# Sums of squares taken along with the first projections, and seven more score units for VectorE

## The chip, the cores and the metric

The kernel runs on one core of a Trainium2 chip. A core has a matrix engine (TensorE, "PE" in the profile, with its weight loads as "PEld"), an elementwise engine (VectorE, "DVE"), an activation engine (ScalarE, "ACT"), a general engine (GpSimd, "POOL") and an engine that only issues transfers (SyncE, "SP"). Each works through its own instructions in order; semaphores join them. Sixteen DMA engines move data between DRAM and the on-chip memory SBUF; products of TensorE land in eight banks of PSUM. The metric is the device time of one execution in microseconds.

## What is computed

Two layers, each an attention block and then a gated block, with a layer norm ahead of each, on x of 2048 tokens by 448 features. Both layers use the same weights.

```python
def _A_ref(x, wqkv, wo):                       # 16 heads of 28
    q, k, v = (x @ wqkv) split into heads
    p = softmax(q k^T * 28 ** -0.5)
    return concat(p v) @ wo
def _B_ref(x, w_gate, w_up, w_down):           # 448 -> 1792 -> 448
    return (sigmoid(x @ w_gate) * (x @ w_up)) @ w_down

x = x + _A_ref(_layernorm(x), wqkv, wo)
x = x + _B_ref(_layernorm(x), w_gate, w_up, w_down)
x = x + _A_ref(_layernorm(x), wqkv, wo)
x = x + _B_ref(_layernorm(x), w_gate, w_up, w_down)
```

## The kernel before, in words

**Numbers in two halves.** The result has to be that of fp32 products. TensorE is given each operand as a high and a low fp16 part, and the products high·high, high·low and low·high are added. So that a weight fits fp16, it is scaled by a power of two that follows from the sum of squares of the whole matrix. These sums are `sums[:, 0:3]` for q, k and v, and `sums[:, 3:7]` for wo, w_gate, w_up and w_down. The first three are taken at the very start. The last four, and the fp16 parts of those four matrices, are needed only behind the first attention.

**Projections** (`project`, L678). Tokens come in four blocks of 512. For a block, `qk` (L691) forms seven tiles of 128 rows of q and k, each a chain of 11 matmuls of 512 columns in one of four PSUM banks in turn (L707). ScalarE and VectorE evacuate a tile: high part (L722), low part (L723), squares (L725) and their pairwise maximum (L727). SP writes the parts to DRAM (L730). Three tiles later TensorE takes the tile's norm products, which read those maxima (L701, L704); `finish` (L736) takes the last three and VectorE reduces the peaks (L740). `vals` (L749) forms the values of a block, four tiles of tokens, evacuated by ScalarE (L758).

The lists given to `qk` (`fill`, L731) and `vals` (`after`) set what is put between the tiles, on whichever engine: one entry behind each tile. Here stands the preparation of later blocks. Blocks 2 and 3 are normalised and transposed in 32 x 32 pieces by VectorE (`squares`), stored to DRAM by SP in pieces of 128 fp32 (`store`, L317, tensor `xt_scr`), read back feature by feature (`gather`, L325, tile `xraw`), and split into high and low by ScalarE and VectorE (`ready`, L210 to L216). In layer 0, block 2 is gathered behind tile 0 of block 1, its split stands behind tile 5 and 6, and block 3 is stored behind tile 6. Block 3 is gathered with the first values of block 1 and split behind tiles 1 and 2 of block 2.

Behind the projections a guard is worked out from the peaks (`guard_of_norms`, L836; `worst_of_heads`, L852). All engines read its flag for a branch, and then the first head's operands are completed (L658) and the attention begins.

**Attention** (`attend`, L1101). Work is in units: one key tile of 128 by 512 queries, so 64 units a head and 1024 in all. TensorE forms a unit's scores (L1129). Most units go in groups of three to ScalarE, which takes their exponential in one instruction (`score`, L1133 to L1144). A few are set aside for VectorE, which takes the exponential with some ten instructions on a polynomial (`score_aside`, L1146 to L1163). `FEW` (L66) says how many of each head of layer 0; a head of layer 1 gives three. `ASIDE` says at which key tile a unit is begun, and which one it is. Then TensorE multiplies the probabilities by the values (`mix`, L1180). Behind each key tile `along` is called with its number c, counted from 0 to 255 over the heads.

**Preparing the later weights** (`Prepare`, L912). From c = 4 of layer 0 on, `Prepare` works through a list of steps, each due at a number c. First come 12 raw tiles of wo, w_down, w_gate and w_up, read from DRAM through GpSimd's queue and summed by VectorE: 19 sums of squares (`add`, L1015 to L1020). Then `sizes` (L1031) reduces them over the partitions on GpSimd and works out the scales. Then the matrices are read a second time and split (`split`, L1040), and the parts go to DRAM. The steps of the sums are due every 4 or 5 key tiles, those of the splits every 7 or 8, and the last at c = 220.

**Buffers.** SBUF is cut into 19 large slots and 12 quarter slots. `big.get` takes the slot that has been free longest, `big.put` gives it back at the end of the list (`Slots`, L75). A tile in a slot waits for whoever used the slot last, whatever that was.

Of the kernel before, what the change touches and what calls it, by code (L numbers as in the profile page):

```python
# [11 lines left out]
F32 = mybir.dt.float32  # L12
# [53 lines left out]
FEW = "2221212111111233"  # L66
# [44 lines left out]
def interleaved_layers(ctx: ExitStack, tc: tile.TileContext, x_in, wqkv, wo, w_gate, w_up,  # L111
# [566 lines left out]
    def project(layer, wq, begun):  # L678
# [12 lines left out]
        def qk(b, blk, fill, before):  # L691
# [16 lines left out]
            for i in range(7):  # L708
# [24 lines left out]
                if i < len(fill) and fill[i]:  # L733
                    fill[i]()
# [150 lines left out]
        return values, heads, last_values  # L885

# [25 lines left out]
    class Prepare:  # L912


        def __init__(self):
            nc.vector.memset(sums[:, 3:7], 0.0)
            self.part = cpool.tile([P, 2], F32, name="part", tag="part", bufs=1)
            self.raws, self.packs = big.ring(2), big.ring(2)
            self.halves, self.half = None, 0
            tiles = [("o", 0)] + [("d", j) for j in range(4)] + [("gu", j) for j in range(7)]  # L920
# [3 lines left out]
            self.read(*tiles[0])  # L924
            self.steps = deque()
            at = 6
            for i, (do, what) in enumerate(order):
                then = order[i + 1][1] if i + 1 < len(order) else None
                self.steps.append((at, lambda do=do, what=what, then=then:
                                   self.step(do, what, then)))  # L930
                at += ((5 if what[0] == "gu" else 4) if do == self.measure else
                       {"o": 5, "w": 8}.get(what[0], 7))
                if i == len(tiles) - 1:
                    self.steps.append((at, self.sizes))
# [12 lines left out]
        def read(self, kind, j):  # L947
# [9 lines left out]
            elif kind == "gu":  # L957
# [836 lines left out]
```

## Time and profile before

| | us |
|---|---|
| median of three runs (lowest, highest) | 1913.93 (1912.98, 1913.96) |
| the profiled execution | 1918.24 |
| its span, first to last instruction | 1916.4 |
| TensorE busy | 1897.9 (99%) |
| VectorE busy | 1412.8 (74%) |
| ScalarE busy | 1366.0 (71%) |
| GpSimd busy | 240.6 (13%) |

The granted clock of TensorE is 0.997 on average over the span. The columns of the profile's rows are explained where they are shown. Matmuls overlap in the pipeline, so the length of one is more than the distance from one to the next, and "busy" is no proof that TensorE does all it could.

### The profile page before, as it was taken

Reading aid. Unit: us, or ns where it says so; the run is one execution under the profiler, and the core shown is the slowest. Engines: PE = TensorE matmul, PEld = TensorE weight load, DVE = VectorE, ACT = ScalarE, POOL = GpSimd, SP = SyncE. Lnnn points to the kernel's source line nnn. Section 1 sums busy time; section 2 is a strip of 40 time slices with the busy share of each in tenths; the row PEclk is TensorE's granted clock in tenths of the full one; section 3 lists DMA queues with packets and bytes.
Section 4 is the critical chain, followed back from the end, with each engine's and each line's share of the span. In section 5 each row is a group of like instructions: output and inputs, shape, how many; then the busy total and the mean of one; then the engine's idle time right before and its main releaser. Section 6 shows DMA issues by size and latency. Waiting matters only on the chain. (4 is left out here: it accounts for less than half of the span.)

```text
span 1916.4 us, 56353 instructions
## 1 busy us (share of the span) xinstructions
PE 1897.9 (99%) x24317; PEld 1405.8 (73%) x24317; DVE 1412.8 (74%) x2816; ACT 1366.0 (71%) x1742; POOL 240.6 (13%) x467
## 2 busy tenths in 40 slices
PE   9999999999999999999999999999999999999999
PEld 4455655555566798999954568778888777899998
DVE  7648798687877598788663487778778667887764
ACT  5569999999983455454344799999999645555541
POOL 2013312232001111212100000000000011211110
PEclk9999999999999999999999999999999999999999
DMA  5575555345313657656634312122111235665752
GB/s 173 165 207 162 155 157 149 117 144 149 92 62 92 235 189 263 219 221 236 232 94 132 89 51 51 28 51 51 41 37 66 75 98 215 216 270 198 270 204 90
DMA packets 107298, 275.20 MB, mean 144 GB/s; under 512 B 12766, under 2 KB 63086, under 8 KB 106912
## 3 DMA queue, kind: packets, MB, share of 16 engines
q0 software_dynamic: 33088, 165.74, 24.5%
q1 hardware_dynamic: 73616, 105.54, 19.3%
q8 instruction: 192, 3.15, 0.7%
q14 instruction: 66, 0.54, 0.1%
q10 hardware_dynamic: 336, 0.23, 0.0%
HBM read 213.39 MB, written 50.73 MB: 138 GB/s over the span
## 5 line engine op out<-in xcount | busy, mean ns | idle before, releaser
L1144 ACT ACTIVATE prob_s<-sc 128x1536 f32<-128x1536 f32 x659 | 892.7, 1484 | 6.7 <-PE sc L1129 3.3
L1180 PE MATMUL acc<-prob_s,val_s 128*32 128x256 f32 (+3 forms) x7754 | 590.1, 383 | 0.0
L1129 PE MATMUL sc<-qp_s 114*32 114x512 f16 x7896 | 575.8, 379 | 0.0
L545 PEld LDWEIGHTS <-gu_s 128*128 128x128 f16 x4368 | 428.0, 98 | 60.3 <-issue 8.1
L1129 PEld LDWEIGHTS <-qp_s 114*32 114x32 f16 x8192 | 309.9, 96 | 176.3 <-issue 78.2
L1180 PEld LDWEIGHTS acc<-prob_s,val_s 128*32 128x32 f32 x7754 | 317.9, 110 | 100.8 <-issue 7.6
L545 PE MATMUL chain<-xwide_s,gu_s 128*128 128x256 f16 x2016 | 249.0, 273 | 4.1 <-DMA gu_s<-gu_parts 4.0
L1454 PE MATMUL dnp<-dn_s,hparts_s 128*128 128x224 f16 x2100 | 235.5, 259 | 0.0
L1454 PEld LDWEIGHTS <-hparts_s 128*128 128x128 f16 x2100 | 202.1, 98 | 4.8
L1527 ACT COPY one_q<-chain 128x256 f32<-128x256 f32 x224 | 82.0, 372 | 132.0 <-PE chain L545 131.3
L1160 DVE SCALAR_TENSOR_TENSOR power_q<-power_q,expo_q 128x512 f32<-128x512 f32 x222 | 153.7, 692 | 7.6
L545 PE MATMUL side<-xshort_s,gu_s 128*128 128x256 f16 x1120 | 142.1, 274 | 3.0 <-DVE one_q L1543 2.7
L530 PE MATMUL qkp<-xhl_s,wqk_s 128*128 128x512 f16 x616 | 138.0, 379 | 0.7 <-DVE xhl_s L509 0.3
L1543 DVE TENSOR_TENSOR one_q<-side,one_q 128x512 f32<-128x512 f32 x112 | 72.0, 684 | 83.4 <-PE side L545 83.4
L530 PEld LDWEIGHTS <-wqk_s 128*128 128x128 f16 x616 | 60.0, 98 | 70.1 <-ACT wqk_s L223 1.0
L1209 DVE STREAM_TRANSPOSE oturned_q<-acc 128x512 f32<-128x512 f32 x32 | 22.9, 717 | 118.4 <-PE acc L1180 118.4
L1345 POOL DMA_DIRECT2D gu_s<-gu_parts x104 | 56.0, 540 | 365.7 <-PE side L545 183.3
L545 PE MATMUL side<-xwide_s,gu_s 128*128 128x256 f16 x672 | 92.3, 274 | 0.0
L1407 ACT CAST hparts_s<-hsums_q 128x256 f16<-128x256 f32 (+1 forms) x144 | 68.4, 489 | 33.1 <-DVE hsums_q L1419 20.6
L722 ACT ACTIVATE qkhl_q<-qkp 128x512 f16<-128x512 f32 x56 | 33.2, 593 | 75.0 <-PE qkp L530 71.6
L1180 PE MATMUL acc<-power_q,val_s 128*32 128x256 f32 (+3 forms) x278 | 86.4, 393 | 0.0
L1554 ACT ACTIVATE one_q<-one_q 128x512 f32<-128x512 f32 x56 | 35.3, 630 | 71.3 <-DVE one_q L1543 71.2
(209 smaller groups left out, 2291.0 us busy)
## 6 DMA issues: line engine op xcount, KB each, us to landing
gu_s<-gu_parts POOLq DMA_DIRECT2D x104, 800.0 KB, 6.0
dn_s<-dn_parts POOLq DMA_DIRECT2D x50, 784.0 KB, 7.2
qp_s<-qk_scr SPq DMA_DIRECT2D x96, 224.0 KB
qk_scr<-qkhl_q SPq DMA_DIRECT2D x56, 256.0 KB
gu_parts<-pack_s POOLq DMA_DIRECT2D x14, 800.0 KB, 4.2
xt_scr<-xs_s SPq DMA_DIRECT2D x48, 224.0 KB
xraw_s<-xt_scr SPq DMA_DIRECT2D x12, 768.0 KB
qp_s<-qk_scr SPq DMA_DIRECT2D x64, 112.0 KB
```

Source lines behind the costliest of these rows:

```text
L530: nc.tensor.matmul(pm, w, x, start=(i == 0), stop=(i == len(terms) - 1))
L545: nc.tensor.matmul(pm, a, x, start=(first and i == 0), stop=(i == len(terms) - 1), skip_group_check=True)
L1129: nc.tensor.matmul(ps[32 * j:32 * j + 32, :], hd.k[:, keys], hd.q[:, qb * W:(qb + 1) * W], start=True, stop=True, tile_position=(0, 32 * j))
L1144: nc.scalar.activation(prob[:, 0:n, :], ps[:, 0:n, :], AF.Exp, scale=exp_scale)
L1160: nc.vector.scalar_tensor_tensor(p, p, c[k], y, op0=ALU.add, op1=ALU.mult)
L1180: nc.tensor.matmul(acc[qb * VC:(qb + 1) * VC, s], v[:, kc % TB, h, :], probs[c * NB + qb][:, s], start=(kc == 0 and a == 0), stop=(kc == N ...
L1345: queue.dma_start(self.gu[-1][m], gu_parts[p, m])
L1407: nc.scalar.copy(to[:, :, 0], a)
L1454: nc.tensor.matmul(pm, a[:, x, t], w[:, p, y], start=(begin and n == 0 and (j == 0 or alone)), stop=(n == 2), skip_group_check=True)
L1527: nc.scalar.copy(to, pm)
L1543: nc.vector.tensor_tensor(one[m], side[m], one[m], op=ALU.add)
L1554: nc.scalar.activation(out, v, AF.Sigmoid, scale=gate_scale)
```

## The change

Three things change, all in layer 0.

- The 19 sums of squares leave `Prepare` for a new class `Measure`, used in `project`. Its raw tiles are read through GpSimd's queue, the first four behind tiles 2 to 5 of block 1, the others as a summed tile is given back. One sum stands behind each of two values tiles of block 1, seven behind the tiles of block 2 (one, one, two, none, none, one, two), seven behind those of block 3, and three behind values tiles of blocks 2 and 3. The split of block 3 moves from behind tiles 1 and 2 of block 2 to behind tiles 3 and 4.
- `Prepare` has only `sizes`, due at c = 6, and the splits from c = 7 on, now 11 key tiles apart for w_down and 10 for w_gate and w_up; the last is due at c = 229.
- `FEW` gives VectorE two units in each of the first 15 heads and three in the last, 33 units where there were 26.

```diff
-FEW = "2221212111111233"
+FEW = "2222222222222223"
...
         if layer == 0:
-            fill = [b2.gather, b3.norm, sq(3, 0, 1), sq(3, 2, 3), idle,
-                    lambda: b2.ready(0, 1), lambda: (b2.ready(2, 3), b3.store())]
+            tell = Measure()
+            read, add = tell.read, tell.add
+            two = lambda: add(2)
+            fill = [b2.gather, b3.norm, (read, sq(3, 0, 1)), (read, sq(3, 2, 3)), read,
+                    (read, lambda: b2.ready(0, 1)), (lambda: b2.ready(2, 3), b3.store)]
...
-        vals(1, b1, {0: b3.gather, 2 if layer == 0 else 1: fin})
-        fin = qk(2, b2, [idle, lambda: b3.ready(0, 1), lambda: b3.ready(2, 3)], None)
-        fin = qk(3, blks[3], [], fin)
+        if layer == 0:
+            vals(1, b1, {0: b3.gather, 1: add, 2: fin, 3: add})
+            fin = qk(2, b2, [add, add, two, lambda: b3.ready(0, 1), lambda: b3.ready(2, 3), add,
+                             two], None)
+            fin = qk(3, blks[3], [add, add, add, add, add, add, add], fin)
...
-        vals(2, blks[2], {0: guard_of_norms, 3: worst_of_heads})
+        after = {2: add} if layer == 0 else {}
+        vals(2, blks[2], {0: guard_of_norms, 3: worst_of_heads, **after})
...
-        vals(3, blks[3], {}, range(2))
+        after = {0: add, 1: add} if layer == 0 else {}
+        vals(3, blks[3], after, range(2))
...
+    class Measure:
+        def __init__(self):
+            nc.vector.memset(sums[:, 3:7], 0.0)
+            self.part = cpool.tile([P, 2], F32, name="part", tag="part", bufs=1)
+            self.junk = big.get("junk", [P, 2048], BF16)
+            self.to_read = deque([("o", 0)] + [("d", j) for j in range(4)] + [
+                ("gu", j) for j in range(7)])
...
+        def read(self):
+            kind, j = self.to_read.popleft()
+            t = big.get("raw", [P, 2048])
+            if kind == "gu":
+                v = t.rearrange("p (w s c) -> p w s c", w=2, s=4)
+                for i, w in enumerate((w_gate, w_up)):
+                    load_rows(v[:, i], w, j * 2 * P, 2 * P, nc.gpsimd)
+                parts = [(4, t[:, 0:1024]), (5, t[:, 1024:2048])]
...
+        def add(self, n=1):
+            for _ in range(n):
+                m, v, t = self.sums.popleft()
+                nc.vector.tensor_tensor_reduce(self.junk[:, 0:v.free_size()], v, v, 1.0,
+                                               sums[:, m:m + 1], op0=ALU.mult, op1=ALU.add,
+                                               accum_out=self.part[:, 0:1])
+                nc.vector.tensor_copy(sums[:, m:m + 1], self.part[:, 0:1])
+                if t is not None:
+                    big.put(t)
+                    if self.to_read:
+                        self.read()
...
-            order = [(self.measure, what) for what in tiles] + [
-                (self.split, what) for what in tiles[:1] + [("w", p) for p in range(NP)] + [
-                    (w, p) for p in range(NP) for w in ("g", "u")]]
...
-                at += ((5 if what[0] == "gu" else 4) if do == self.measure else
-                       {"o": 5, "w": 8}.get(what[0], 7))
+            order = [("o", 0)] + [("w", p) for p in range(NP)] + [
+                (w, p) for p in range(NP) for w in ("g", "u")]
+            self.read(*order[0])
+            self.steps = deque([(6, self.sizes)])
+            at = 7
+            for what, then in zip(order, order[1:] + [None]):
+                self.steps.append((at, lambda what=what, then=then: self.step(what, then)))
+                at += {"o": 5, "w": 11}.get(what[0], 10)
```

More of the change, by code (lines that the diff above doesn't have):

```diff
@@ L733, in qk @@
                 if i < len(fill) and fill[i]:
-                    fill[i]()
+                    for do in fill[i] if isinstance(fill[i], tuple) else (fill[i],):
+                        do()
             def finish():
@@ L988, in view, with step @@
             return t[:, 0:4 * D].rearrange("p (s n) -> p s n", s=4)
-        def step(self, do, what, then):
+        def step(self, what, then):
             raw = self.next
@@ L994, in step @@
                 self.read(*then)
-            do(raw, *what)
+            self.split(raw, *what)
             if what == ("w", 0):
@@ L1013, in add_up @@
             return s12, s34
-        def add(self, m, v):
-            junk = big.at(self.packs, "junk", [P, 2048], BF16)
-            n = v.free_size()
-            nc.vector.tensor_tensor_reduce(junk[:, 0:n], v, v, 1.0, sums[:, m:m + 1],
-                                           op0=ALU.mult, op1=ALU.add, accum_out=self.part[:, 0:1])
-            nc.vector.tensor_copy(sums[:, m:m + 1], self.part[:, 0:1])
-        def measure(self, raw, kind, j):
-            if kind == "o":
-                self.add(3, raw[:, 0:4 * D])
-            elif kind == "gu":
-                self.add(4, raw[:, 0:1024])
-                self.add(5, raw[:, 1024:2048])
-            else:
-                self.add(6, raw[:, 0:self.count(j) * D])
         def sizes(self):
```

47 lines of the change are left out of this document (22 added, 25 removed).

## The prediction

> **What bounds the kernel now.** I read the page first, then the busy time of the two attention stages, then the first projections row by row in order of time, then the DMA groups. In the rows of stretches stand start:end, length, the busy time (and instruction count) of TensorE, its weight loads, VectorE, ScalarE and GpSimd, the granted clock, the DMA share and GB/s.
>
> ```profile
> span 1916.4 us, 56353 instructions
> PE 1897.9 (99%) x24317; PEld 1405.8 (73%) x24317; DVE 1412.8 (74%) x2816; ACT 1366.0 (71%) x1742; POOL 240.6 (13%) x467
> ```
>
> ```profile
> 119.90:570.85 450.95, 450.91 (x8132) 259.31 (x8121) 362.83 (x702) 448.63 (x333) 95.06 (x155) 1.00 0.48 141
> 1069.30:1515.30 446.00, 446.00 (x8097) 357.08 (x8089) 343.92 (x572) 444.04 (x326) 0.00 (x0) 1.00 0.18 46
> ```
>
> TensorE is busy everywhere, so its average tells little. In both attentions ScalarE is full too. Layer 0 runs 333 exponentials of up to three score units each; layer 1, which gives three units of every head to VectorE, runs 326, and is 4.95 us shorter. Per head (one stretch of one head, then of two, five and seven):
>
> ```profile
> 208.36:237.11 28.75, 28.75 (x529) 16.95 (x525) 18.89 (x35) 28.75 (x23) 8.27 (x13) 1.00 0.54 148
> 153.29:208.36 55.07, 55.03 (x995) 33.32 (x989) 48.57 (x89) 54.97 (x42) 22.06 (x37) 1.00 0.59 157
> 320.14:461.64 141.50, 141.50 (x2572) 78.91 (x2564) 110.21 (x233) 141.42 (x106) 42.69 (x72) 1.00 0.48 147
> 1101.35:1295.42 194.07, 194.07 (x3540) 144.82 (x3532) 151.69 (x252) 194.07 (x143) 0.00 (x0) 1.00 0.18 45
> ```
>
> Heads 7 to 11, with one unit, take 28.30 us each. Heads 1 and 2, with two, take 27.54, although the sums of squares bring VectorE to 88% there. Heads 1 to 7 of layer 1, with three, take 27.72: more units buy no more, TensorE has become the floor.
>
> The first projections are another stage:
>
> ```profile
> 58.00:72.00 14.00, 14.00 (x74) 7.13 (x73) 9.15 (x20) 6.63 (x13) 0.00 (x0) 1.00 0.87 245
> 72.00:92.00 20.00, 20.00 (x99) 9.44 (x97) 11.02 (x24) 11.82 (x21) 0.00 (x0) 1.00 0.47 151
> 92.00:107.00 15.00, 15.00 (x77) 7.40 (x76) 6.14 (x17) 6.68 (x11) 0.45 (x1) 1.00 0.35 112
> 148.00:152.00 4.00, 4.00 (x80) 2.27 (x72) 0.91 (x1) 4.00 (x4) 0.19 (x1) 1.00 1.00 368
> 205.00:217.00 12.00, 12.00 (x215) 8.10 (x209) 8.49 (x17) 12.00 (x10) 7.39 (x12) 1.00 0.68 193
> ```
>
> From 58 to 107 TensorE has no gap, VectorE works 26.3 of 49 us, and the DMA engines are 87% busy in the first 14. The last two rows are in the attention, where the weights are read for their sums today: w_down at 368 GB/s with full engines, gate and up at 193/0.68 = 284 GB/s of full engines.
>
> **The change part by part.**
>
> *Attention of layer 0: 33 units to VectorE instead of 26.* Eight heads go from one to two, one from three to two. ScalarE then has 991 units, 331 exponentials instead of 333, the last with one unit instead of two: 7/3 of a group. A group takes 450.95/333 = 1.35 us, so 3.1 us are saved. The other bound is layer 1's pace, 4.95 us; the two-unit heads above (27.54) are already there, but their number is only two, so I keep to 3.1. VectorE bears it: 88% busy held that pace, and the splits now come every 10 or 11 key tiles instead of every 7 or 8. More load could also cost; heads 1 and 2 are the nearest row and speak against it.
>
> *The sizes move from head 3 to head 0.* They bring a stall:
>
> ```profile
> 232.97 0.44 POOL L1032 PARTITION_ALL_REDUCE size<-sums  x1 [6.84 <-issue]
> 233.45 0.17 DVE L238 TENSOR_SCALAR pw<-size 128x4 int32<-128x4 int32 x1 [6.15 <-POOL size L1032]
> ```
>
> VectorE waits 6.15 us, and queued behind it are a head's score units and finish. Head 3, where it is now, took 28.75, that is 0.45 us over heads 7 to 11. In head 0 the second unit is needed six key tiles after it is begun (six sixteenths of 28.3 us), so the bounds are 0 and about 0.5; as this cost is paid today too, I take nothing.
>
> *The 19 sums move into the projections, on VectorE.*
>
> ```profile
> L1018 DVE CUSTOM_DVE_ANT_0 junk_s<-raw_s,sums x19: 1145/1285/2085, 142.7 to 225.8; 128x1024 bf16<-128x1024 f32 x14, 128x1792 bf16<-128x1792 f32 x4, 128x896 bf16<-128x896 f32 x1
> ```
>
> ```profile
> 224.26 1.28 DVE L1018 CUSTOM_DVE_ANT_0 junk_s<-raw_s,sums 128x1024 bf16<-128x1024 f32 x1
> ...
> 225.81 1.29 DVE L1018 CUSTOM_DVE_ANT_0 junk_s<-raw_s,sums 128x1024 bf16<-128x1024 f32 x1
> ```
>
> ```profile
> 49.86 0.65 DVE L723 SCALAR_TENSOR_TENSOR qkhl_q<-qkp,qkhl_q 128x512 f16<-128x512 f32 x1
> 50.43 0.27 DVE L727 TENSOR_TENSOR sq_q<-sq_q 128x256 bf16<-128x256 bf16 x1
> 50.62 0.68 DVE L723 SCALAR_TENSOR_TENSOR qkhl_q<-qkp,qkhl_q 128x512 f16<-128x512 f32 x1
> ...
> 66.71 0.41 DVE L740 TENSOR_REDUCE peaks<-qnorm 16x1 f32<-16x256 f32 x1
> ...
> 78.44 1.29 DVE L211 TENSOR_TENSOR xhl_s<-xraw_s,xhl_s 128x512 f16<-128x512 f32 x2 [3.47 <-ACT xhl_s L210]
> ...
> 104.36 0.29 DVE L727 TENSOR_TENSOR sq_q<-sq_q 128x256 bf16<-128x256 bf16 x1
> ```
>
> One sum with its read-out and copy takes 1.55 us of VectorE (224.26 to 225.81); by its extra 0.27 a long one takes 2.35 (2.085 + 0.27), the short one 1.42. An evacuation pair takes 0.76 (49.86 to 50.62), two peaks 0.8, the four subtractions of block 3 2.6. In the changed order VectorE is free for the first sum at 66.71. Up to the last maximum (L727) of block 3 it then does four long sums (9.4), the short one (1.42), ten of 1.55 (15.5), fourteen pairs (10.64), block 3's subtractions (2.6) and two blocks' peaks (1.6): 41.2 us, so it is done at 107.9; today that is 104.65. Who waits:
>
> ```profile
> 85.60 4.91 PE L530 MATMUL qkp<-xhl_s,wqk_s 128*128 128x512 f16 x22
> ...
> 105.17 0.49 PE L704 MATMUL knorm<-sq_q,ind 128*128 128x256 bf16 x3
> ```
>
> TensorE comes to the norm product of that tile at 105.17 and would wait 2.7 us, in order, with the rest of the values and the attention behind it. Before that the four banks cover VectorE's lag: by the same sum, a tile's evacuation ends about 2 us before its bank is wanted.
>
> *Their reads move too, on GpSimd's queue.* The raw tiles are 128 x 2048 fp32 at most: wo 0.92 MB, w_down 3.2, gate and up 7 times 1.05, in all 11.5 MB. In the changed order the first four reads are queued behind the norm of block 3. I followed the free list of the 19 buffers by hand: reads one to five wait for nothing, six and seven for buffers that are free by 61 and 67, the eighth for the buffer that block 3's store reads. So seven reads (3.67 + 0.46 + 2.1 MB) run into this:
>
> ```profile
> 54.81 1.01 POOL L285 TENSOR_TENSOR rs<-rs,nhalf 128x4 f32<-128x4 f32 x1
> ```
>
> ```profile
> 65.56 3.43 SPq L317 DMA_DIRECT2D xt_scr<-xs_s  x4
> 72.30 0.38 SPq L325 DMA_DIRECT2D xraw_s<-xt_scr  x1
> ```
>
> ```profile
> 77.79 1.14 ACT L210 CAST xhl_s<-xraw_s 128x512 f16<-128x512 f32 x2 [3.15 <-DMA xraw_s<-xt_scr]
> ```
>
> Block 3's store is issued at 65.56 and has landed at 72.30, when its gather is issued; the gather lands 5.5 us later, at 77.79. In the changed order the gather is wanted by ScalarE after tile 3 of block 2: three tiles of 4.91/2 us ahead of 85.60, and an evacuation later, so about 79.5. It has less than 2 us to spare. What a second queue does to transfers, the up reads alone (first row) and beside a head's loads (second row), the last column in us to landing:
>
> ```profile
> raw_s<-in_B_w_up_dram POOLq DMA_DIRECT2D x2, 384.0 KB, 5.3
> ```
>
> ```profile
> raw_s<-in_B_w_up_dram POOLq DMA_DIRECT2D x1, 384.0 KB, 10.3
> ```
>
> Twice as long: equal shares. From 58 on SP's queue has 0.87 x 14 = 12.2 us of full engines to do until its store has landed; GpSimd's seven reads are 3.67/368 + 0.46/368 + 2.1/284 = 18.6 us. The store lands between 72.3 (no contention) and 58 + 12.2 + 18.6 = 88.8 (everything else first). I take equal shares, the row that is nearest: 58 + 2 x 12.2 = 82.4, the gather at 87.9. Block 3's projection then starts 0.65 later (77.79 to 78.44 above), at 88.5 instead of 85.60. VectorE has two subtractions done at 89.8 and still owes 1.3 for the other two, ten of the pairs (7.6), nine sums of 1.55 (13.95) and 0.8 for peaks, together some 23.6: 113.4. TensorE, 2.9 late, waits there until 113.4: 8.2 us behind today. The guard's way (peaks, bound, flag, reload of the guard) is behind by about as much and does not end last. A wait of TensorE also costs clock:
>
> ```profile
> 1582.75 1.56 PE L545 MATMUL side<-xshort_s,gu_s 128*128 128x256 f16 x10 [1.95 <-DVE one_q L1543]
> ```
>
> ```profile
> 1582.00:1590.00 8.00, 7.25 (x34) 3.83 (x34) 7.67 (x17) 3.47 (x7) 1.72 (x4) 0.79 0.08 14
> ```
>
> After a wait of 1.95 us the granted clock was 0.79 for 8 us, which is 1.7 us. I add it once.
>
> *Sum.* +8.2 + 1.7 - 3.1 = +6.8 us. The profiled execution took 1918.24 us (span 1916.4), 4.3 above the median of the three runs, 1913.93; differences are added to the median: 1920.7.
>
> **The rivals.**
>
> *The store comes last (A).* Its pieces are 512 bytes (128 fp32 of one row), those of the weights 1 KB and more. If engines take turns piece by piece, the small pieces fall behind and the store lands at 88.8, 6.4 us after my case: 14.6 + 1.7 - 3.1 = +13.2, 1927.1. For it: the share 0.87 with small pieces. Against: the up read was only doubled. [...]
>
> *The reads are hidden (B).* If they yield to the store, only VectorE's 2.7 us remain, with or without 1.7 of clock: -0.4 to +1.3, about 1914.5. For it: DMA at 47% and 35% after 72. Against: 11.5 MB need some 37 us of full engines in a stage of 49 that already uses 27.
>
> *Faster (C).* Attention 0 reaches layer 1's pace, because VectorE is rid of the sums, and the projections cover theirs: -4.95, 1909.0. It decides if they lose less than 1.1 us. For it: heads 1 and 2 at 27.54. Against: VectorE's own 41.2 us between 66.71 and 105.17.
>
> **How the numbers follow.** Mine 0.38, A 0.25, B 0.2, C 0.13, something else on the slow side 0.04. Within 0.2% is 3.8 us, about what a measurement can tell from no change. Slower by more than that: mine, A and the rest, less 0.02 of mine that would fall within 0.2%: 0.65. Same: B and those 0.02, 0.22. Faster: C, 0.13. Predicted is 1920.7. The range leaves out most of C below and the worst above: 1911 to 1929. For slower alone it is 1918 to 1929.
>
> **What would show it.** Right: an idle TensorE before block 3's first tile with the gather of xt_scr as releaser, waits of the norm products for the maxima, the first exponential some 10 us later than today, and 331 exponentials in layer 0 at 1.35 us or less. Wrong: the gather of block 3 still landing near 78, or sums that start late without TensorE waiting. The forecast fails if the reads yield to the store, or if the free list sets the reads off later than I worked out.

## The result and the profile after

The changed kernel takes 1933.91 us (median of four runs, 1931.22 to 1935.80), the kernel before beside it 1913.45: a ratio of 1.0106, with a 95% interval of 1.0088 to 1.0123. The forecast was 1920.7, with 1929 as the upper end. The direction was right, the size was not: 20.5 us were lost where 6.8 were forecast.

The profiled execution took 1933.51 us. The page's head, and then stretches of it in the columns of the prediction: attention 0, from its end to attention 1, attention 1, the rest, and two pieces of the projections.

```profile
span 1931.0 us, 56368 instructions
...
PE 1897.8 (98%) x24285; PEld 1415.6 (73%) x24285; DVE 1450.8 (75%) x2886; ACT 1362.0 (71%) x1740; POOL 238.8 (12%) x467
```

```profile
138.35:585.07 446.72, 446.72 (x8096) 260.14 (x8089) 373.51 (x714) 444.64 (x331) 64.05 (x107) 1.00 0.38 113
585.07:1084.46 499.39, 492.89 (x4025) 390.55 (x4027) 350.83 (x766) 232.06 (x535) 69.37 (x147) 1.00 0.55 188
1084.46:1530.20 445.74, 445.74 (x8096) 365.98 (x8089) 343.77 (x571) 443.85 (x326) 0.00 (x0) 1.00 0.19 46
1530.20:1931.00 400.80, 390.12 (x3498) 340.64 (x3496) 282.00 (x616) 180.61 (x446) 56.13 (x117) 0.99 0.54 195
60.00:80.00 20.00, 14.80 (x68) 7.04 (x67) 12.52 (x22) 6.36 (x12) 8.50 (x14) 0.83 1.03 362
...
117.00:138.00 21.00, 16.79 (x81) 7.52 (x84) 8.46 (x24) 3.36 (x7) 4.15 (x5) 0.84 0.68 166
```

The first profiled execution of the kernel before (span 1916.4) was longer than most of its others, so I set the stages against a second one, whose span of 1912.7 is the usual one:

```profile
120.18:570.74 450.56, 450.56 (x8128) 261.25 (x8121) 362.79 (x702) 448.45 (x333) 94.69 (x155) 1.00 0.48 141
570.74:1067.99 497.25, 491.31 (x4025) 389.82 (x4026) 351.02 (x766) 232.18 (x535) 69.33 (x147) 1.00 0.55 189
1513.92:1912.70 398.78, 390.30 (x3498) 340.69 (x3496) 282.23 (x616) 180.61 (x446) 56.11 (x117) 1.00 0.54 196
```

The account of the 18.3 us between these two spans: the first exponential comes 18.2 us later (138.35 against 120.18), attention 0 is 3.8 us shorter, the stretch behind it 2.1 longer, attention 1 the same (445.74 against 445.93), the rest 2.0 longer. The stretch behind each attention holds a gated block, whose instructions the change does not touch; the prediction has no term for them.

The 18.2 us, row by row in order of time (start, length, engine, line, operation; in brackets the idle time before it and what ended it):

```profile
65.54 1.14 ACT L210 CAST xhl_s<-xraw_s 128x512 f16<-128x512 f32 x2 [6.58 <-DMA xraw_s<-xt_scr]
...
68.67 10.94 SPq L317 DMA_DIRECT2D xt_scr<-xs_s  x4
...
71.07 0.63 ACT L725 ACTIVATE sq_q<-qkhl_q 128x512 bf16<-128x512 f16 x1 [3.90 <-DMA qk_scr<-qkhl_q]
71.73 0.29 DVE L727 TENSOR_TENSOR sq_q<-sq_q 128x256 bf16<-128x256 bf16 x1 [3.65 <-ACT sq_q L725]
72.08 0.37 PE L704 MATMUL knorm<-sq_q,ind 128*128 128x256 bf16 x1 [5.20 <-DVE sq_q L727]
...
87.04 0.38 SPq L325 DMA_DIRECT2D xraw_s<-xt_scr  x1
...
92.25 1.14 ACT L210 CAST xhl_s<-xraw_s 128x512 f16<-128x512 f32 x2 [5.15 <-DMA xraw_s<-xt_scr]
...
115.07 0.27 PE L704 MATMUL knorm<-sq_q,ind 128*128 128x256 bf16 x1 [0.53 <-DVE sq_q L727]
...
117.26 0.37 PE L704 MATMUL knorm<-sq_q,ind 128*128 128x256 bf16 x1 [1.92 <-DVE sq_q L727]
117.42 0.58 PE L555 MATMUL vp<-wv_s,xhl_s 128*128 128x448 f16 x1
...
125.17 0.20 PE L864 MATMUL bounds<-ident,bnd 16*1 16x16 f32 x2
...
127.30 1.28 DVE L938 CUSTOM_DVE_ANT_0 junk_s<-raw_s,sums 128x1024 bf16<-128x1024 f32 x1
...
133.60 0.36 PE L555 MATMUL vp<-wv_s,xhl_s 128*128 128x448 f16 x1 [3.96 <-DVEq L877]
```

- *A quarter slot.* ScalarE waits 6.58 us for block 2's gather, and the evacuation of block 1's last tile is queued behind the split. Then it is to write the squares of that tile (`sq_q`) into a quarter slot, but the slot still holds parts (`qkhl_q`) that are on their way to DRAM. With the DMA engines full (1.03 in 60 to 80) both transfers land late; ScalarE, VectorE and TensorE wait one behind the other, TensorE 5.20 us at the tile's norm product, and its clock falls (0.83). This place is not in the prediction. (Expectations below put it in block 2; the norm product stands among the values of block 1.)
- *Block 3.* Its store is issued at 68.67 and has landed at 87.04; the gather lands at 92.25. TensorE is 7.7 us late at block 3's start in any case (93.30 against 85.60), so this costs only some 1.5 us more.
- *The norm products of block 3.* 0.53 and 1.92 us, together 2.45.
- *The branch.* Two sums stand in VectorE's program behind the flag and ahead of the flag's reading (L877). TensorE waits 3.96 us for them. This place is not in the prediction either.

With TensorE's rows set against those of the second execution of before, the 18.2 us are 0.2 from before 60 us, 7.3 at the quarter slot, 1.5 at block 3, 4.0 at the norm products and 5.2 at the branch; all but block 3's have a stretch of lower clock in them.

For the first and the last place, the same rows of the kernel before:

```profile
66.02 0.49 PE L704 MATMUL knorm<-sq_q,ind 128*128 128x256 bf16 x3
...
111.83 0.20 PE L854 MATMUL bounds<-ident,bnd 16*1 16x16 f32 x2
...
112.27 0.20 DVE L856 TENSOR_SCALAR flag<-worst,back 1x1 int32<-1x1 f32 x1
...
116.93 0.35 PE L555 MATMUL vp<-wv_s,xhl_s 128*128 128x448 f16 x1 [0.63 <-ACT val_s L758]
```

The flag is ready at 112.47, and TensorE is through the branch at 116.93, 4.46 us later, held by a bank and not by the flag. So the way from VectorE through the branch takes at most 4.5 us there, and TensorE's two value tiles cover it. In the changed kernel VectorE is 2.97 us later than its flag (125.81 to 128.78), and that is more than the cover. From the bounds to the first exponential the kernel before takes 8.15 us (111.83 to 119.98), the changed one 13.18.

### The profile page after: what moved, and what is told of

The parts are those of the page before. It is cut to its first block, busy times and chain, and to the rows that moved or that the text cites. A ratio compares the mean times of both kernels' runs of the same rounds, so it can differ in the third digit from the quotient of the medians.

```text
span 1931.0 us, 56368 instructions
## 1 busy us (share of the span) xinstructions
PE 1897.8 (98%) x24285; PEld 1415.6 (73%) x24285; DVE 1450.8 (75%) x2886; ACT 1362.0 (71%) x1740; POOL 238.8 (12%) x467
## 5 line engine op out<-in xcount | busy, mean ns | idle before, releaser
L1168 ACT ACTIVATE prob_s<-sc 128x1536 f32<-128x1536 f32 (+1 forms) x657 | 888.5, 1484 | 11.6 <-DMA qp_s<-qk_scr 8.1
L1184 DVE SCALAR_TENSOR_TENSOR power_q<-power_q,expo_q 128x512 f32<-128x512 f32 x243 | 168.2, 692 | 8.3
L1204 PE MATMUL acc<-power_q,val_s 128*32 128x256 f32 (+3 forms) x300 | 94.2, 396 | 0.0
```

What stands on the lines that cost most here:

```text
L1168: nc.scalar.activation(prob[:, 0:n, :], ps[:, 0:n, :], AF.Exp, scale=exp_scale)
L1184: nc.vector.scalar_tensor_tensor(p, p, c[k], y, op0=ALU.add, op1=ALU.mult)
L1204: nc.tensor.matmul(acc[qb * VC:(qb + 1) * VC, s], v[:, kc % TB, h, :], probs[c * NB + qb][:, s], start=(kc == 0 and a == 0), stop=(kc == N ...
```

## The experiments

All ran beside the kernel before. "Gated" is the span less the first exponential's start and the two attentions, in the profiled execution; in the two of the kernel before it is 899.6 and 896.0.

| run | median (lowest, highest) us | ratio (95%) | first exp. | attention 0 | gated |
|---|---|---|---|---|---|
| after_again | 1935.70 (1934.60, 1936.79) | 1.0103 (1.0088, 1.0118) | 138.18 | 446.79 | 903.7 |
| few_only | 1931.35 (1930.45, 1931.81) | 1.0082 (1.0065, 1.0099) | 121.62 | 461.24 | 900.6 |
| sums_only | 1933.70 (1932.38, 1935.03) | 1.0092 (1.0075, 1.0109) | 138.64 | 450.53 | 898.5 |
| no_reads | 1922.45 (1916.24, 1923.37) | 1.0031 (1.0018, 1.0043) | 127.63 | 446.11 | 901.0 |
| tiny_sums | 1923.14 (1919.09, 1931.12) | 1.0045 (1.0030, 1.0060) | 127.41 | 446.74 | 898.0 |
| past_branch | 1928.56 (1925.90, 1928.58) | 1.0063 (1.0047, 1.0079) | 130.69 | 447.06 | 901.7 |
| sq_apart | 1931.09 (1927.09, 1931.72) | 1.0074 (1.0057, 1.0091) | 135.65 | 446.15 | 901.5 |
| hybrid | 1918.99 (1914.94, 1923.33) | 1.0020 (1.0009, 1.0030) | 120.00 | 449.15 | 900.3 |
| hybrid2 | 1919.30 (1913.34, 1924.86) | 1.0025 (1.0013, 1.0038) | 119.74 | 446.90 | 899.2 |
| before_shift | 1919.85 (1916.71, 1923.11) | 1.0026 (1.0013, 1.0039) | 120.33 | 450.57 | 901.4 |
| after_shift | 1931.11 (1928.32, 1933.38) | 1.0088 (1.0074, 1.0102) | 136.70 | 446.76 | 899.8 |
| hybrid2_shift | 1914.87 (1912.40, 1919.81) | 1.0006 (0.9997, 1.0015) | 120.53 | 446.92 | 902.9 |
| hybrid3 | 1910.92 (1909.19, 1918.31) | 0.9979 (0.9968, 0.9991) | 120.25 | 446.85 | 896.4 |

**One part alone.** In the kernel before, the list of units only:

```diff
-FEW = "2221212111111233"
+FEW = "2222222222222223"
```

> The kernel before with only the new list of units for VectorE (two in each of the first 15 heads, three in the last). Sums and splits stay where they were in the kernel before. Theory (the loss of the change arises ahead of the attention, and the units are a gain): the first exponential starts where it starts before, at 119.98, and attention 0 shrinks by 3.1 to 4.2 us; 1909.3 to 1910.4. Rival (the units cost where VectorE also carries sums and splits at the old distances, so heads 1 to 3 slow down): attention 0 shrinks by less than 1 us or grows; 1913 or above.

```profile
121.62:582.86 461.24, 451.81 (x8096) 272.59 (x8089) 405.49 (x772) 445.50 (x331) 94.56 (x155) 0.99 0.46 138
377.40:411.32 33.92, 30.53 (x572) 17.79 (x565) 32.97 (x68) 32.40 (x25) 10.58 (x18) 1.00 0.48 149
```

The rival holds, at another place: attention 0 grows by 10.7 us over the second execution of before, and not in heads 1 to 3 but in heads 9 and 12, with 33.9 us each; in head 9 VectorE is 97% busy (32.97 of 33.92), and ScalarE stands still 5.6 us in the head behind it. The sums are over by then (the last at 225.8 in the kernel before); these are heads in which VectorE has the splits. Why heads 4 to 8, with the same units, do not stall is not shown. In the changed kernel, with the sums gone and the splits further apart, the same list gives 446.72. And the other half, the changed kernel with the old list:

```diff
-FEW = "2222222222222223"
+FEW = "2221212111111233"
```

> The changed kernel with the old list of units (26 instead of 33); sums in the projections and the wider spacing of the splits as changed. Theory: the whole loss of the projections without the gain of the units, 3.1 to 4.2 us above the changed kernel: 1937 to 1938; first exponential near 138.4. Rival (part of the loss is made by the units beside the splits, since the two profiled executions lie only 15.3 us apart and the medians 20.5): 1929 to 1934.

Attention 0 takes 450.53 us, what it takes before: taking the sums out gains nothing there by itself. Neither part pays alone, both together give 3.8 us. The time, however, is not 3.8 us longer: 1933.70 against 1933.91 and 1935.70 for the changed kernel. So the rival holds by its number, but not by its reason, for the attention does show the gain of the units. The gated blocks make up for it (898.5 against 900.2 and 903.7), which is the question of the last experiments.

**Transfers or VectorE.** First without the reads (the same sums run over `x`), then without most of the sums' elements:

```diff
-                    load_rows(v[:, i], w, j * 2 * P, 2 * P, nc.gpsimd)
...
-                parts = [(4, t[:, 0:1024]), (5, t[:, 1024:2048])]
+                parts = [(4, xf[:, 0:1024]), (5, xf[:, 1024:2048])]
```

```diff
                 m, v, t = self.sums.popleft()
+                v = v[:, 0:8]
```

> The changed kernel with the raw tiles left unread: the 19 sums run at the same places and over the same numbers of elements, but over x, so wo, w_down, w_gate and w_up get other scales. VectorE's work is the same, the 11.5 MB of transfers are gone. Theory (transfers and VectorE each hold a share): block 2's gather lands near 62.4 again, no quarter slot is late, block 3's gather lands near 78; what stays is the wait of the norm products of block 3 (about 2.7 us), the wait at the branch behind the two last sums (about 3.3 us) and the lower clock after them (about 1.5 us each). First exponential 7 to 10 us later than before, time 1917 to 1920. Rival V (VectorE's work alone makes the loss): 1930 to 1934. Rival D (the transfers alone make it): 1909 to 1911.

> The changed kernel with all reads as they are, but each sum taken over 8 columns of its tile only (so the four scales are other ones): VectorE's work falls by about 25 us, the transfers stay. Theory: the late gather of block 2, the wait for a quarter slot and the late block 3 stay (8 to 10 us), the norm products of block 3 and the branch wait less than 1 us; first exponential 8 to 12 us later than before, time 1917 to 1922. Rival V: 1909 to 1911. Rival D: 1930 to 1934.

TensorE's waits of more than 0.5 us from 40 us on to the attention, all there are, first without reads, then with tiny sums:

```profile
107.05 0.27 PE L704 MATMUL knorm<-sq_q,ind 128*128 128x256 bf16 x1 [0.87 <-DVE sq_q L727]
...
122.50 0.55 PE L555 MATMUL vp<-wv_s,xhl_s 128*128 128x448 f16 x1 [4.55 <-DVEq L877]
```

```profile
70.61 0.37 PE L704 MATMUL knorm<-sq_q,ind 128*128 128x256 bf16 x1 [4.64 <-DVE sq_q L727]
...
124.35 0.35 PE L555 MATMUL vp<-wv_s,xhl_s 128*128 128x448 f16 x1 [0.63 <-ACT val_s L759]
```

Both theories of one cause fall. VectorE's work alone makes the branch late and costs 7.5 us at the first exponential; the transfers alone make the quarter slot late and cost 7.2, a little less than the 8 to 12 expected. Together it is 18.2, 3.5 more than the sum. Both times lie above their ranges, by 2.5 and 1.1 us. The wait for the norm products in block 3 is only 0.87 us where the reads are gone: VectorE's last maximum ends at 107.0 (forecast 107.9) and TensorE comes to it at 106.2 (forecast 105.17). The 2.45 us of the changed kernel are partly the reads' doing. In tiny_sums two short sums, 0.8 us, stand behind the flag as well, and from the bounds to the first exponential it is 8.15 us as before: so much is covered.

**Each wait by itself.** The two last sums behind the branch, and the squares in a slot of their own:

```diff
-        after = {0: add, 1: add} if layer == 0 else {}
-        vals(3, blks[3], after, range(2))
+        vals(3, blks[3], {}, range(2))
         if layer == 0:
-            assert not tell.sums
+            owed.extend([add, add])
...
+            if layer == 0 and c in (1, 3):
+                owed.popleft()()
```

```diff
+            sqs = big.get("sqs", [P, 8, W], BF16)
...
-                sq = qrt.get("sq", [P, W], BF16)
+                    sq = sqs[:, taken[0] % 8]
```

> The changed kernel once more, on the chip of the next three runs, so that they can be set against it directly. The three waits found in its trace (the norm product in block 2 behind a quarter slot, 5.20 us; block 3's norm products, 2.45 us together; the branch behind the two last sums, 3.96 us) should come back at the same places and the time at 1931 to 1936. If the waits move about from execution to execution, the places differ.

> The changed kernel with its two last sums moved from behind the flag's computation into head 0 of the attention (behind key tiles 1 and 3). Theory: VectorE reads the flag at once, TensorE does not wait at the branch (3.96 us) and its clock does not fall behind it (1.8 us); the two sums, 3.1 us, fit into the 10.4 us in which VectorE has nothing to do in head 0. 1928 to 1929, that is 5 to 6 us less than the changed kernel. Rival (what is waited for at the attention's start is the first head's operands from DRAM, late by themselves): less than 2 us gained, 1932 or above.

> The changed kernel with the squares of blocks 1 to 3 in one large slot of their own instead of quarter slots, so that a tile of squares no longer takes the slot of a tile whose parts are still on their way to DRAM. The reads stay, with one large slot fewer free for them. Theory (late transfers hold two places one behind the other): the wait of 5.20 us in block 2 is gone, but block 3 still begins when its gather has landed, near 95, and the time falls by no more than 2 us: 1932 to 1934. Rival (the quarter slot is the loss, block 3 would be on time): about 7 us less, 1926 to 1928.

The waits of the changed kernel came back in its second run at the same places (4.61, 0.53 and 1.92 us). With the two sums behind the branch:

```profile
116.10 0.27 PE L706 MATMUL knorm<-sq_q,ind 128*128 128x256 bf16 x1 [1.92 <-DVE sq_q L729]
116.21 0.35 PE L555 MATMUL vp<-wv_s,xhl_s 128*128 128x448 f16 x1
...
122.54 0.20 PE L866 MATMUL bounds<-ident,bnd 16*1 16x16 f32 x2
...
130.69 1.45 ACT L1169 ACTIVATE prob_s<-sc 128x1536 f32<-128x1536 f32 x1 [3.11 <-DMA qp_s<-qk_scr]
```

From the bounds to the first exponential it is 8.15 us, to the hundredth what the kernel before takes, and 7.1 us come off the median of after_again. 5.0 of them are the branch with the lower clock behind it (13.18 less 8.15); in this trace the clock does not fall behind the norm products either. With the squares apart:

```profile
83.39 0.38 SPq L325 DMA_DIRECT2D xraw_s<-xt_scr  x1
...
88.98 0.38 PE L530 MATMUL qkp<-xhl_s,wqk_s 128*128 128x512 f16 x1 [2.54 <-ACT xhl_s L210]
...
113.36 0.27 PE L705 MATMUL knorm<-sqs_s,ind 128*128 128x256 bf16 x1 [1.94 <-DVE sqs_s L733]
```

Of the 5.20 us of wait 0.79 are left, and what comes out is close to the prediction's own case: the store has landed at 83.39 (forecast 82.4), block 3 begins at 88.98 (88.5), the last norm product stands at 113.36 (113.4). Part of that is luck: one large slot is gone, so six reads and not seven run ahead of the store's landing, and the store is issued 1.7 us later (67.26 against 65.56). TensorE now waits 2.54 us for block 3, and the time falls by 4.6 us at the median (2.5 at the first exponential), between the two expectations: about half of the quarter slot's 5.20 us comes back as the next wait.

**The same parts, placed elsewhere.** Reads of wo and w_down during block 0; tiles of gate and up held until block 3's gather has landed; the rest in head 0; nothing behind the flag.

```diff
+            def gate():
+                nc.gpsimd.tensor_copy(tell.part[:, 1:2], b3.raw[:, 0, 0:1])
+            fill = [idle, idle, lambda: b1.norm([0, 1]), (lambda: b1.norm([2, 3]), read), read,
+                    (scaled, read), (read, read)]
...
+            vals(1, b1, {0: b3.gather, 1: add, 2: fin, 3: (lambda: (add(), gate(), read()))})
+            fin = qk(2, b2, [(add, read), (add, read), add, lambda: b3.ready(0, 1), lambda: b3.ready(2, 3), add,
+                             add], None)
+            fin = qk(3, blks[3], [add, add, add, add], fin)
...
+            tiles = [("gu", j) for j in range(3, 7)]
```

> The kernel before with the new list of units, and the 19 sums in three lots: wo and w_down read during block 0 (where the transfers are 36% busy) and summed from block 1's values on; three tiles of gate and up read only once block 3's gather has landed, six sums ahead of block 3's tile 4; the last four tiles with eight sums in head 0, three key tiles apart, sizes behind them, splits 10 key tiles apart. Nothing stands between the flag and the branch. Theory (the three waits are made by the place of reads and sums, and the units pay where VectorE has room): first exponential at 120 to 121.5, attention 0 at 447 to 448: 1910 to 1913, below the kernel before by 1.5 to 4. Rival (VectorE at 26.3 of 49 us has no room for sums in the projections wherever they stand; or head 0 pays for eight sums): 1915 or above.

The first exponential is at 120.00: 11 sums and 8 reads cost the projections nothing. But head 0 has eight sums and takes 34.99 us, ScalarE stands still 2.0 us in heads 1 and 2, and attention 0 gains only 1.4. At 1918.99 us the time misses the theory's 1910 to 1913; the rival's second reason, that head 0 pays for eight sums, is there. hybrid2 has five tiles of gate and up in the projections, two of the sums in VectorE's gaps around the guard; against hybrid:

```diff
-            fin = qk(3, blks[3], [add, add, add, add], fin)
+            fin = qk(3, blks[3], [add, add, add, add, add, add], fin)
...
                                            op1=ALU.mult)
+            if layer == 0:
+                add()
             nc.gpsimd.tensor_tensor(bnd, bnd, half[0:H, 0:1], op=ALU.pow)
```

> As the run with three lots of sums (hybrid), but 15 instead of 11 sums stand in the projections: four more behind tiles 3 to 6 of block 3 and in the two gaps of VectorE around the guard, where it waited 2.4 us each; head 0 has only four sums, four key tiles apart, from key tile 8 on. Theory (in that run heads 0 to 2 were held by VectorE, 96% and more busy, and the projections lost nothing): first exponential at 120 to 121, heads 0 to 2 as in the changed kernel (32.5, 27.5, 28.0), attention 0 at 446 to 447, 3 us less than that run: 1914 to 1916. Rival (its loss against the kernel before lies elsewhere, in what follows the attention): no change, 1918 to 1920.

The stages do as the theory says (119.74, 446.90), the median does not move. So the rival holds for the time: the rest of the loss lies in what follows.

**The gated blocks.** The kernel before once more:

> The kernel before once more, one look. Its first profiled execution took 1918.24 us, above nearly all its other times (median 1914.6), so stages compared with it come out too small by some 4 us somewhere. If the stage in question is the projections or the attention of layer 0, this look shows a first exponential before 118 or an attention 0 below 449; if it is one of the two gated blocks (498.50 us between the two attentions, 401.1 behind the second), they are shorter here by that amount.

It is the gated blocks: 896.0 where the first execution had 899.6; the other stages agree within 0.4 us. The clock makes this difference. It falls to 0.50 for 3.41 us at a time, three times in the gated blocks of the first execution and once in those of the second (the last 2 us left out), and each time costs 1.7 us of full clock. One such stretch of the first execution, and the same one in the second:

```profile
638.17:641.58 3.41, 2.94 (x13) 1.83 (x13) 3.41 (x8) 1.35 (x3) 0.00 (x0) 0.50 0.02 9
```

```profile
638.17:641.58 3.41, 2.95 (x20) 1.94 (x20) 3.41 (x8) 1.34 (x3) 0.00 (x0) 1.00 0.02 9
```

These stretches come with waits of TensorE (in the first execution of before one begins at 1675.82, behind a wait of 2.06 us that ends at 1675.29; in the changed kernel one at 744.92, behind 3.48 us that end at 744.22), and not in the same places in every execution. They also go with the spread: the twelve times of hybrid2 run from 1913.34 us at a clock of 0.999 to 1924.86 at 0.994. So one profiled execution cannot give the price of what follows; the medians have to.

Some 160 us into each block TensorE waits for a load of weights (`gu_s`) that is issued under other transfers. In the executions up to hybrid2 that wait is 1.6 to 2.2 us with the old list and 2.2 to 3.5 with the new one, and the load takes 6.9 to 7.2 against 7.3 to 8.5. The load's issue and the wait, first in the second execution of before, then in the changed kernel, and the changed kernel's DMA queues in that stretch (packets, MB, share of 16 engines):

```profile
722.28 0.53 POOL L1345 DMA_DIRECT2D gu_s<-gu_parts  x1 [9.17 <-DMA xt_scr<-xs_s]
...
729.42 0.83 PE L545 MATMUL chain<-xwide_s,gu_s 128*128 128x256 f16 x6 [1.99 <-DMA gu_s<-gu_parts]
```

```profile
735.65 0.53 POOL L1369 DMA_DIRECT2D gu_s<-gu_parts  x1 [9.23 <-DMA xt_scr<-xs_s]
...
744.22 0.83 PE L545 MATMUL chain<-xwide_s,gu_s 128*128 128x256 f16 x6 [3.48 <-DMA gu_s<-gu_parts]
```

```profile
q0 software_dynamic: 308, 1.76, 55.1%
q1 hardware_dynamic: 480, 0.92, 32.5%
q8 instruction: 1, 0.02, 0.8%
q14 instruction: 1, 0.01, 0.2%
```

In the changed kernel one packet of each of two instruction queues falls into the load; before, none (the queue rows of that stretch are q0 and q1 alone). The packet of queue 8 takes 0.8% of 16 x 8.6 us, 1.1 us of one engine. In the whole first trace of before queue 8 has 192 packets (the page: 3.15 MB, so 16 KB each) for TensorE's 48,634 rows, one for 253. With the old list the 79th of them stands at nearly the same row in all three executions, ahead of this load (19,749th and 19,745th row in the two executions of before, 19,751st in sums_only); with the new list the 79th lies inside it, at the 19,798th. The new list takes 64 of these rows away (24,285 matmuls and as many weight loads, instead of 24,317), so the load stands elsewhere between the packets. Whether a packet makes the load longer into which it falls can be tried by moving nothing but the number of TensorE's instructions ahead of it. Only the matmuls that keep TensorE busy at the start (`keep_busy`) are cut finer, with nearly the same columns in sum (at least 510 of 512): into six for before_shift (190 more instructions, 63 short of the 253 from one packet to the next, where the new list takes 64 away), into three or four for after_shift and hybrid2_shift (64 more).

```diff
-        for i in range(n):
+        for i in range(k * n):
             c = slice(P * (i % 4), P * (i % 4) + P)
-            nc.tensor.matmul(pm, still[:, c], still, start=(i == 0), stop=(i == n - 1))
+            nc.tensor.matmul(pm[:, 0:W // k], still[:, c], still[:, 0:W // k], start=(i == 0),
+                             stop=(i == k * n - 1))
```

> [...] Theory I (the 1.3 us longer weight loads of the gated blocks in all kernels with the new list come from a 16 KB instruction packet that falls into them, because the packets stand at fixed counts of TensorE's instructions): TensorE's wait near 160 us into each gated block rises from 2.0 to 3.0 to 3.5 us, the gated blocks take 899 to 903 us together instead of 896 to 899, and the time is 3 to 5 us above the kernel before, less what the start costs. Rival (something else of the new list, or chance): waits at 2.0 and the gated blocks as in the kernel before.

> The changed kernel with the warming matmuls at the start cut so that TensorE's program is 64 instructions longer, as many as the new list of units takes away, so that the instruction packets stand in the gated blocks where they stood in the kernel before. Theory I: the waits near 160 us into the gated blocks go back to about 2.0 us and the time falls by 2 to 5 us, to 1930 to 1933. Rival: no change, 1934 to 1936.

> The kernel with 15 sums in the projections in three lots and the new list of units (hybrid2), with TensorE's program 64 instructions longer at the start in the same way. That kernel's profiled execution took 1913.54 us, its median 1919.30, between 1913.3 and 1924.9, with the granted clock between 0.999 and 0.994. Theory I: waits in the gated blocks at 2 instead of 3 to 3.5 us, so fewer executions lose clock behind them; median 1911 to 1914, the first kernel below the one before. Rival: no change, 1917 to 1920.

The kernel before, with its packets moved:

```profile
721.35 0.53 POOL L1346 DMA_DIRECT2D gu_s<-gu_parts  x1 [9.24 <-DMA xt_scr<-xs_s]
...
729.96 1.25 PE L546 MATMUL chain<-xwide_s,gu_s 128*128 128x256 f16 x5 [3.55 <-DMA gu_s<-gu_parts]
```

```profile
q8 instruction: 1, 0.02, 0.8%
```

The wait is 3.55 us, and the median rises by 6.1 us over before (ratio 1.0026, 1.0013 to 1.0039) with first exponential and attention as they were. Theory I holds here. For after_shift it is not shown: the median is 4.6 us below after_again, but only 2.8 below the changed kernel's first 1933.91, the intervals of the ratios overlap (1.0088 to 1.0118, 1.0074 to 1.0102), and 1.5 us lie ahead of the first exponential. For hybrid2_shift the median falls by 4.4 us (ratio 1.0025 to 1.0006, the intervals overlap a little), between the two expectations; its traced execution is one of its longest, with four stretches of half clock in the gated blocks where the one of hybrid2 has one, so that its 902.9 in the table says nothing against it. In both the waits fall only to 2.95 and 2.90: the load still takes 8.0 and 7.8 us. There the packet of queue 8 lies ahead of the load, and one of queue 14 (8 KB) inside it. 24 tiny fills by VectorE move that one:

```diff
+            if layer == 0 and 226 <= c < 250:
+                nc.vector.memset(prepare.part[:, 1:2], 0.0)
```

> hybrid2_shift with 24 tiny fills by VectorE (128 x 1) in heads 14 and 15, where it waits some 10 us a head. There the 16 KB packet lay ahead of the weight load again, but a second kind of packet, 8 KB, of another queue, now lay inside it (6.3 and 3.5 us behind its issue), and the load took 7.75 us instead of 7.1. If that packet is VectorE's and stands at a fixed count of its instructions, 24 more put it some 10 us earlier, ahead of the load. Theory I for this queue as well: the load takes 7.0 to 7.3 us, the waits near 160 us go to 2.0, the gated blocks to 893 to 896, the time to 1909 to 1912, below the kernel before (1913.8). Rival: load, waits and time as in hybrid2_shift, 1914 to 1916.

```profile
720.35 0.53 POOL L1412 DMA_DIRECT2D gu_s<-gu_parts  x1 [9.28 <-DMA xt_scr<-xs_s]
...
727.27 0.83 PE L546 MATMUL chain<-xwide_s,gu_s 128*128 128x256 f16 x6 [1.89 <-DMA gu_s<-gu_parts]
```

The load takes 6.9 us, the wait is 1.89, the gated blocks take 896.4 us, and the time is 1910.92 us, 0.9979 of the kernel before (0.9968 to 0.9991). In the second gated block the load takes 7.3 us and the wait is 2.38. No packet lies inside either load; the one of queue 14 now begins 5.6 us ahead of the first, at VectorE's 1,196th row; in hybrid2_shift it stood at the 1,193rd. Over all sixteen traces and both blocks this load takes 6.9 to 7.3 us where no instruction packet begins inside it and 7.3 to 8.6 where one or more do. A second wait, near 69 us into the last gated block, moves the same way (1.94 us in the second execution of before and in hybrid3, 2.65 in before_shift, 3.00 in the changed kernel); what makes it was not followed.

This is the one version that beats both. Its projections and attention:

```profile
60.00:80.00 20.00, 20.00 (x102) 9.82 (x101) 19.08 (x34) 10.37 (x19) 1.11 (x3) 1.00 0.79 229
80.00:100.00 20.00, 20.00 (x98) 9.48 (x97) 19.46 (x46) 11.53 (x20) 16.35 (x28) 1.00 0.99 323
```

```profile
120.25:567.10 446.85, 446.85 (x8096) 266.06 (x8089) 380.83 (x750) 444.71 (x331) 69.63 (x117) 1.00 0.41 121
```

VectorE works 38.5 of 40 us and TensorE does not wait: 15 of the 19 sums did fit into the projections, at other places than the change gave them.

## Why the prediction was right or wrong

- *Attention 0, -3.1 us: right.* It is -3.8. Its reason, that heads 1 and 2 at 88% speak against a cost of more load, was too kind: few_only shows that with sums and splits at the old distances the same list costs 10.7 us, in heads that have the splits. That the splits come further apart, which the prediction names, was the condition and not a help; hybrid, with splits 10 key tiles apart, has no stall in heads 9 and 12.
- *Sizes in head 0, nothing: right.* Head 0 takes 32.5 us in the changed kernel (138.35 to 170.80), 32.9 to 33.3 before.
- *VectorE's 2.7 us at the norm product, and 5.3 of wait with block 3 late (113.4 less 105.17 and 2.9): place right, sizes too large.* Without the reads it is 0.87, in the changed kernel 2.45, in sq_apart 1.94, because TensorE comes later than worked out.
- *"I take equal shares", store landed at 82.4, block 3 at 88.5: nearly right for a kernel without the quarter slot* (sq_apart: 83.4, 88.98, and 113.36 against 113.4, with one read fewer). The free list was right: the eighth read waits for block 3's store. In the changed kernel the store is issued 3.1 us late and has landed at 87.04, nearer to rival A's 88.8.
- *"Seven reads run into this", with the store as the one victim: this step failed.* Every transfer on SP's queue in that time was a victim, the gather of block 2 and the writes of q and k parts as well, and one of these held a quarter slot that the last tile of block 1 needed. I followed the 19 large slots by hand and not the 12 quarter slots. It cost 7.3 us before block 2's first tile, and block 3's delay then cost only 1.5.
- *"The guard's way ... does not end last": this step failed too.* I counted the peaks, the bound and the flag, and not the two sums between the flag and the branch. The rows of before gave a warning: flag at 112.47, branch passed at 116.93, and TensorE stood still only 0.63 us there, for a bank. It cost 5.0 us (13.18 less 8.15).
- *"I add it once": the clock, 1.7 us, was sized too small.* It fell at three places: behind the quarter slot's wait (0.83 in 60 to 80), behind the norm products and behind the branch (0.84 in 117 to 138). That is 3.4 us each for the two stretches, 6.8 in all.
- *Nothing was said of the gated blocks.* They cost 4 us in the profiled execution and some 6 by the medians (20.5 less 18.2, plus 3.8); the prediction treated work that the change does not touch as unchanged in time. No row of before could give the price, but the page has the 192 packets, and the trace has a load that TensorE waits for.
- *Rivals.* A (1927.1) was nearest, but by luck: the store's landing, its one reason, cost only 1.5 us. Its 88.8 lets every read land first; 83.39 in sq_apart and 87.04 in the changed kernel lie between that and equal shares. Its condition, that engines take turns piece by piece, is shown by no run. B's bare projections are no_reads, and even these lose 7.5 us at the first exponential. C's premise, that the projections can cover the sums, is shown by hybrid3 for 15 of them.

## What to carry to other kernels

When transfers are moved, list every transfer under way in the new stretch, and for each the buffers that wait for it, small ones too; the latest of them sets the time, and removing it shows the next. Before work goes behind a flag or another short chain, read in the trace what covers that chain now and by how much. And when a change of a fraction of a percent shows up in stages whose code is the same, compare the places of the instruction packets and the stretches of lower clock before looking for a cause in the code, over several executions and not over one.

## What the runs showed of the hardware

- An instruction packet of 16 KB beside a load of 0.8 MB made the load 1.5 us longer (7.1 in before, 8.6 in before_shift, where it is the only one), one of 8 KB (queue 14: 66 packets, 0.54 MB on the page of before) 0.7 to 0.9 us (7.1 to 7.8 in hybrid2_shift and 8.0 in after_shift). Moving the packets alone changed the median of the kernel before by +6.1 us, of hybrid2 by -4.4 and, with the second queue, of hybrid2_shift by -4.0 more. The runs show where the packets lie and what the load takes, not by what way the one lengthens the other.
- The clock fell by half for 3.41 us at a time, or twice that (0.50 in 69.08 to 75.91 of the changed kernel), and not by the length of a wait alone: after the same wait of 1.92 us the next matmul took 0.58 us in the changed kernel (row at 117.42) and 0.35 in past_branch (row at 116.21), and in the first execution of before the clock stayed at 1.00 behind a wait of 1.98 us (ended at 730.78) and fell behind one of 1.95 (ended at 1582.75). What decides it no run shows.
- From VectorE's last instruction ahead of the branch to TensorE behind it took 4.8 us (from 128.78, the end of the last sum's copy, to 133.60) to 5.3 us (sq_apart, 125.09 to 130.40) where TensorE was held by it. Where TensorE was not held, it was at most 4.5 us in the kernel before (112.47 to 116.93) and at most 3.7 in tiny_sums (120.68 to 124.35). Why a held TensorE takes longer is open.
